# Reordered expert products around chunk 1, and a split store of the last rows, in a fused attention and expert kernel

## The chip, the cores and the metric

The kernel runs on one core of a Trainium2 chip. The metric is the device time of one execution in microseconds. Before the change its median is 507.99 us over six executions (506.37 to 508.11).

## The reference

Attention over pooled keys and values, followed by a mixture of four experts that are all computed for every row:

```python
# q, k, v: (8 batches, 8 heads, 576 rows, 64); pool = 8, so 72 pooled keys
k_p = k.reshape(B, H, 72, 8, D).mean(axis=3)
v_p = v.reshape(B, H, 72, 8, D).mean(axis=3)
attn = softmax(q @ k_p.T / 8)
x = (attn @ v_p), heads side by side        # (4608, 512)
p = domain_probs / domain_probs.sum(-1)     # (4608, 4)
for e in range(4):                          # w1: (4, 512, 1024), w2: (4, 1024, 512)
    out += p[:, e:e+1] * (relu(x @ w1[e]) @ w2[e])
```

## The kernel before

**Chunks and steps.** The 4608 rows are cut into nine chunks of 512: chunk c below 8 is the first 512 rows of batch c, and chunk 8 collects the last 64 rows of every batch. A step is one chunk with one expert; `steps` lists them, chunk by chunk, expert by expert, and the loop over s (L946) has one pass more than steps. In pass s the up products (x times w1, then relu) of step s are written out together with the down products (hidden times w2) of step s-1. Hidden values stand transposed, `H_sb`, in two buffers; the sums over experts stand in `accs`, one tile per 128 rows.

**Forms.** `up_plain` (L658) makes an up product in 8 column blocks of 4 matmuls with 512 columns. `up_seven` (L718) makes it by Strassen's scheme from seven products of half the size (`product`, L641: four matmuls of 256 columns into one of the three banks `g`, `d`, `s` of `psum_h`); ScalarE keeps a partial sum in `r` (L691), VectorE adds it and applies the relu (L695), and ScalarE does a relu alone (L698). `up_down` (L776) puts both the up and the down product into that scheme, from step (1, 2) on. The scheme needs sums of weights (`combine_w1` L595, `combine_w2` L627, four operations on VectorE each, for the expert named) and of inputs (`forms_of`, L606). `down` (L848) is the plain down product: 8 matmuls of 512 columns for each of four row blocks, in pieces n = 0 to 3 of 3, 4, 5 and 4 matmuls for each half j, and then `merge` (L865) multiplies by the probability and adds, on VectorE (L872), into `acc`.

**Pass 4** (s == E, L1006) stands between the last step of chunk 0 and the Strassen steps of chunk 1: chunk 1's first up product is plain. For j = 0 it does the four down pieces; for j = 1 each down piece is followed by two of the eight up blocks.

**Order.** All engines run in the order in which the code is written (`manual_schedule`, L893). Work for the next batch's attention is dropped into it at numbered points: every `between` or `up_down` counts through `point` (L935), 16 points a pass, and `placed` holds what is due at each. At a `slot` (L941) also the next entry of `forms_due` is taken, which is where the sums of weights go. `second_attention` (L516) is the plan of batch 1 during chunk 0, by point number: fold the keys (L203, VectorE), transpose them (`second_keys`, L315, PE, then an ACT copy), transpose the queries in two halves (`second_queries`, L322, PE, then a VectorE copy), four `scores` (L263, PE, then an exp on ACT, L276), two halves of `fold_values` (L246), four `context` (L400, PE, then reciprocal and `x_tok` on VectorE, L376 and L377), each with its `turn` (L418), a DMA transpose from SP's queue that writes a quarter of xT. `attention(c)` (L539) is the plan of batch c+1 during chunk c, in the same way.

**Banks.** `psum_a` holds one tile of two banks, which key and query transposes, scores and contexts of batches 1 to 7 take in turn: each waits until the one before has been read. `psum_h` and `psum_o` have three banks each. For batch 0, `attention_first` (L489) and `turn_here` (L423) use transposes on PE; there two row blocks share one `psum_a` tile, and a copy on ACT (L432) takes each out.

**Loads and stores.** The inputs are loaded from POOL's queue, in code order; all but the probabilities are cast to bf16 on the way. `store` (L880) writes a finished row block from SP's queue; for chunk 8 these are two transfers of 64 rows, since a row block holds rows of two batches. Pass 36 has only the down products of the last step and these stores (L990 to L992).

Of the kernel before, what the change touches and what calls it, by code (L numbers as in the profile page):

```python
# [13 lines left out]
BF16 = mybir.dt.bfloat16  # L14
F32 = mybir.dt.float32
# [3 lines left out]
def kernel(  # L19
# [10 lines left out]
    nc = tc.nc  # L30

    B, H, S, D = q.shape
# [78 lines left out]
    def load_q(b):  # L111
        q_sb = qpool.tile([P, H, NR, D], BF16, name="q_sb")
        nc.gpsimd.dma_start(
            out=q_sb[:].rearrange("p h r d -> p h (r d)"),
            in_=q[b, :, 0:NT, :].rearrange("h (p r) d -> p h (r d)", r=NR),
        )
        raws[("q", b)] = q_sb
# [22 lines left out]
    def load_v(b):  # L140
        load_kv(b, v, "vraw")
# [281 lines left out]
    def turn_here(b, r):  # L423
        if r == 0:
            state[("xT", b)] = xpool.tile([P, KC, NT], BF16, name="xT")
        if r % 2 == 0 or b:
            state["xt_ps"] = psum_a.tile([P, 2, KC, P], BF16, tag="a", name="xt_ps")
        xt_ps = state["xt_ps"][:, r % 2]
        flat = state.pop(("x", b, r))[:].rearrange("p a h d -> p (a h d)")
        for kc in range(KC):  # L430
            nc.tensor.transpose(xt_ps[:, kc, :], flat[:, kc * P:(kc + 1) * P], ident[:])
        nc.scalar.copy(out=state[("xT", b)][:, :, r * P:(r + 1) * P], in_=xt_ps)  # L432

    def rem_queries(i):
        q_rem = q_rems.pop(i)
# [80 lines left out]
    def second_attention():  # L516

        lo, hi = halves

        return {  # L520
            42: [lambda: fold_keys(1, lo)],
            44: [lambda: fold_keys(1, hi), lambda: load_k(2)],
            47: [second_keys],
            50: [lambda: second_queries(0)],
            51: [lambda: second_queries(1), lambda: load_q(2), lambda: load_q_rem(2)],
            53: [lambda: scores(1, 0)],
            55: [lambda: scores(1, 1)],
            56: [lambda: fold_values(1, lo)],
            57: [lambda: scores(1, 2)],
            58: [lambda: fold_values(1, hi)],  # L530
            59: [lambda: scores(1, 3)],
            60: [lambda: context(1, 0), lambda: turn(1, 0)],
            61: [lambda: context(1, 1), lambda: turn(1, 1)],
            62: [lambda: context(1, 2), lambda: turn(1, 2)],
            63: [lambda: context(1, 3), lambda: turn(1, 3)],
            64: [lambda: load_v(2)],
        }

    def attention(c):  # L539

        lo, hi = halves
        b = c + 1
        plan = {}

        def add(n, *what):
            plan.setdefault(n, []).extend(what)

        if c % 2:
            i = c // 2
            q_at = 15 if b < B else 2  # L550
            for n, piece in zip((0, 8, 11, 12), (rem_queries, rem_scores, rem_context, rem_turn)):
                add(q_at + n, lambda piece=piece: piece(i))
        parts = forms_of(b, nc.gpsimd)
        add(25, *parts)
        if b == B:
            return plan
        more, far = b + 1 < B, b + 2 < B
        if c == 1:
            add(0, lambda: queries(b), *key_parts(b)[:2])
            add(1, *key_parts(b)[2:])  # L560
            add(1, lambda: keys(b), lambda: loads_wait(b))
            add(1, lambda: (load_q(b + 1), load_q_rem(b + 1)))
            for pair in range(NPAIR):
                add(7 + pair, lambda pair=pair: scores(b, pair))
            for n, part in enumerate(value_parts(b)):
                add(6 + n, part)
            mixed = (11, 12, 13, 14)
        else:
            for pair in range(NPAIR):
                add(2 + 2 * pair, lambda pair=pair: scores(b, pair))  # L570
            for n, part in enumerate(value_parts(b)):
                add(4 + n, part)
            mixed = (9, 11, 12, 19)
        for n, r in zip(mixed, range(NR)):
            add(n, lambda r=r: context(b, r))
            add(n + 1, lambda r=r: turn(b, r))
        if more:
            add(4, lambda: load_half(b + 1, k, "kraw", 0))
            add(11, lambda: queries(b + 1))
            add(8, lambda: load_half(b + 1, k, "kraw", 1))  # L580
            add(16, *key_parts(b + 1))
            add(21, lambda: load_half(b + 1, v, "vraw", 0))
            add(27, lambda: load_half(b + 1, v, "vraw", 1))
            add(24, lambda: keys(b + 1))
        if far:
            add(28, lambda: (load_q(b + 2), load_q_rem(b + 2)))
        return plan
# [259 lines left out]

    def down(c, e, j, n):  # L848

        first = (0, 3, 7, 12, 16)  # L850
        for at in range(first[n], first[n + 1]):
            r, fc = 2 * j + at // FCH, at % FCH
            if fc == 0:
                sums[r] = psum_o.tile([P, DM], F32, name="o_ps")
            nc.tensor.matmul(  # L855
                sums[r][:], lhsT=hidden[(c, e)][:, fc, r * P:(r + 1) * P], rhs=w2_bf[:, e, fc, :],
                start=(fc == 0), stop=(fc == FCH - 1),
            )
            if fc == FCH - 1:
                if held is not None and r == NR - 1:  # L860
                    held.append(lambda: merge(c, e, r, sums[r]))
                else:
                    merge(c, e, r, sums[r])

    def merge(c, e, r, o_ps):  # L865
        prob = p_all[:, c * NR + r, e:e + 1]
# [10 lines left out]
            return  # L877
        store(c, r)

    def store(c, r):  # L880
        dst = accs[(c, r)][:]
        if c < B:
            rows = out[c * S:c * S + NT, :].rearrange("(p r) d -> p r d", r=NR)
            nc.sync.dma_start(out=rows[:, r, :], in_=dst)
        else:
            for bb in range(2):
                at = (2 * r + bb) * S + NT
                nc.sync.dma_start(out=out[at:at + REM, :], in_=dst[bb * REM:(bb + 1) * REM])

    zeros = x_rem[:, 0]  # L890
    pool_map = x_rem[0:FR, 1, 0:FT * SP].rearrange("p (r j) -> p r j", r=FT)
# [1 line left out]
    with tc.manual_schedule(engines={ENG.PE, ENG.DVE, ENG.Activation, ENG.Pool, ENG.SP}):  # L893
# [52 lines left out]
        for s in range(len(steps) + 1):  # L946
# [17 lines left out]
            if s == 1:  # L964
                w, u, x = combine_w2(0), combine_w1(0), forms_of(0)
                forms_due.extend([lambda w=w, u=u, n=n: (w[n](), u[n]()) for n in range(3)])
                forms_due.extend(nothing[:1] + combine_w1(2))
                for part in x[:3]:
                    part()
            elif s == 2:  # L970
                x[3]()
                forms_due.extend(nothing + combine_w1(3))
            elif s == 4:
                v2, x = combine_w2(1), forms_of(1)
                forms_due.extend(v2[:2] + combine_w1(1))
                forms_due.extend([lambda: (x[0](), x[1]()), lambda: x[2]()])
            elif s == 5:
                x[3]()
                forms_due.extend(u[3:] + nothing[:2] + combine_w2(2))
            elif s == 6:  # L980
                v3 = combine_w2(3)
                forms_due.extend(nothing[:1] + v3[:1] + nothing[:2] + v3[1:])
            elif s == 7:
                forms_due.extend(nothing[:1] + v2[2:3] + nothing[:3] + v2[3:])
            elif s == 8:
                forms_due.extend(nothing[:1] + w[3:])
            elif s == E * B + 1:
                reload_w2(E - 1)
            for j in range(2):
                if not live:  # L990
                    for n in range(4):
                        between(j, n)  # L992
                elif s == 0:
                    for i in range(4):
                        up_half(j, i)
                        if j == 0 and i in (1, 2):
                            turn_here(0, i + 1)
                        if j == 0 and i == 2:
                            norm_probs()
                        between(j, i)  # L1000
                elif s == 1:
                    for n in range(4):
                        between(j, n)
                    for n in range(4):
                        up_plain(c, e, [4 * j + n])
                elif s == E:  # L1006
                    for n in range(4):
                        between(j, n)
                        if j:
                            up_plain(c, e, [2 * n, 2 * n + 1])  # L1010
                elif splits(*steps[s - 1]):
                    up_down(c, e, j, *steps[s - 1])
                else:
                    up_seven(c, e, j, lambda n: between(j, n))
# [30 lines left out]
```

## Time and profile before

| | us |
|---|---|
| median of six executions | 507.99 |
| the six | 506.37, 506.74, 507.95, 508.04, 508.07, 508.11 |
| the profiled execution | 508.07 |
| its span, first to last instruction | 506.4 |
| PE busy / VectorE busy / ACT busy / POOL busy | 493.6 / 354.9 / 287.2 / 180.0 |
| first matmul of pass 36 (at 494.7) to the end of the span | 11.7 |
| DMA bytes | 41.90 MB |

Busy times are sums over the span; PE's includes the drawn ends of pipelined matmuls, which overlap the next one. A line of the timeline gives start, duration, engine, source line, operation, what it writes and reads, shape and count of equal instructions in a row; brackets give the idle time of the engine before it and what ended that. The table by stretches gives the busy time of each engine from one time to another, the clock granted to PE, the share of the DMA engines and the rate of the transfers.

### The profile page before, as it was taken

What the parts mean: (1) busy time and instruction counts of PE and PEld (TensorE: products, weight loads), DVE (VectorE), ACT (ScalarE), POOL (GpSimd) and SP (SyncE); (2) the same over time, 40 slices, a digit from 0 to 9 for tenths busy, and PEclk for the clock granted to TensorE, in tenths of its full rate; (3) what the DMA queues carried; (4) which work ended last, traced back from release to release, by engine and by line L of the source; (5) the groups of instructions that cost most, each with busy time, mean ns of one, the idle gap of its engine ahead of it and who ended that gap; (6) DMA issues with size and microseconds to landing.
All of it is one profiled execution on the core that took longest, in us unless ns stands there. A gap on an engine that the chain in (4) does not pass through costs nothing.

```text
span 506.4 us, 10931 instructions
## 1 busy us (share of the span) xinstructions
PE 493.6 (97%) x4468; PEld 392.9 (78%) x4483; DVE 354.9 (70%) x650; ACT 287.2 (57%) x531; POOL 180.0 (36%) x165
## 2 busy tenths in 40 slices
PE   8899889999999999999999999999999999999996
PEld 3656544667888888888888888888888888888883
DVE  2363879677777776777777777777877766776674
ACT  3554343745576557655766576556655565556650
POOL 8372102144522671266126722661115111512110
PEclk9899999999999999999999999999999999999999
DMA  9999997991837355844673286333200110012003
GB/s 132 205 206 206 201 147 153 122 112 15 87 103 98 48 55 122 109 49 47 122 108 53 19 123 118 51 45 62 64 18 16 43 43 12 2 43 63 2 1 83
DMA packets 83506, 41.90 MB, mean 83 GB/s; under 512 B 46576, under 2 KB 78832, under 8 KB 83456
## 3 DMA queue, kind: packets, MB, share of 16 engines
q0 software_dynamic: 42112, 22.91, 35.2%
q1 hardware_dynamic: 41344, 18.29, 17.0%
q8 instruction: 35, 0.57, 0.4%
q14 instruction: 15, 0.12, 0.1%
HBM read 45.69 MB, written 9.44 MB: 109 GB/s over the span
## 4 chain that ended last, share of the span: by engine, by line
PE 91%; DVE 5%; ACT 2%; DMA 1%; issue 1%; ACTq 0%; POOLq 0%
PE g_ps L647 38%; PE u_ps L769 35%; PE o_ps L855 8%; PE h_ps L665 3%; PE two L272 2%; PE h_ps L678 2%; PE two L395 1%; DVE H_sb L695 1%; DMA H_sb<-in_k_dram 1%; DVE x_tok L377 1%; DVE acc L872 1%; DVE acc L753 0%; PE o_ps L487 0%; ACT expT L357 0%; ACT xT L432 0%
## 5 line engine op out<-in xcount | busy, mean ns | idle before, releaser
L647 PEld LDWEIGHTS <-w_bf 128*128 128x128 bf16 x1848 | 177.4, 98 | 27.9 <-issue 2.5
L753 DVE SCALAR_TENSOR_TENSOR acc<-u_ps,p_all,acc 128x512 f32<-128x512 f32 (+1 forms) x204 | 121.3, 594 | 77.0 <-ACT u_ps L806 72.7
L715 POOL TENSOR_TENSOR h_s<-H_sb,h_s 128x1024 bf16<-128x1024 bf16 x29 | 61.5, 2120 | 236.3 <-DVE h_s L714 236.3
L647 PE MATMUL g_ps<-xT,w_bf 128*128 128x256 bf16 x928 | 130.0, 273 | 0.0
L647 PE MATMUL g_ps<-xf,w_bf 128*128 128x256 bf16 x792 | 109.8, 272 | 0.6 <-ACT g_ps L790 0.4
L691 ACT COPY r<-g_ps 128x512 f32<-128x512 f32 x140 | 81.9, 585 | 46.4 <-PE g_ps L647 41.8
L695 DVE CUSTOM_DVE_ANT_0 H_sb<-g_ps,r 128x512 bf16<-128x512 f32 x140 | 96.3, 688 | 13.4 <-ACT r L691 8.7
L769 PEld LDWEIGHTS <-H_sb 128*128 128x128 bf16 x928 | 86.7, 98 | 18.3 <-DVE H_sb L713 4.7
L769 PE MATMUL u_ps<-w_bf,H_sb 128*128 128x256 bf16 x696 | 95.3, 273 | 0.4 <-DVE H_sb L713 0.3
L698 ACT ACTIVATE H_sb<-g_ps 128x512 bf16<-128x512 f32 x124 | 74.0, 597 | 20.6 <-PE g_ps L647 20.6
L769 PEld LDWEIGHTS <-h_s 128*128 128x128 bf16 x696 | 68.1, 98 | 7.9
L790 ACT COPY g_ps<-g_ps 128x512 f32<-128x512 f32 x58 | 33.1, 570 | 65.3 <-PE g_ps L647 65.3
L769 PE MATMUL u_ps<-w_t,h_s 128*128 128x256 bf16 x464 | 69.6, 273 | 0.0
L855 PE MATMUL o_ps<-w_bf,H_sb 128*128 128x512 bf16 x213 | 53.2, 379 | 0.6
L806 ACT COPY u_ps<-u_ps 128x256 f32<-128x256 f32 x58 | 20.7, 357 | 32.9 <-PE u_ps L769 32.7
L855 PEld LDWEIGHTS <-H_sb 128*128 128x128 bf16 x224 | 21.8, 98 | 18.9
L769 PE MATMUL u_ps<-w_t,H_sb 128*128 128x256 bf16 x232 | 34.9, 273 | 0.0
L769 PE MATMUL u_ps<-w_bf,h_s 128*128 128x256 bf16 x232 | 34.8, 273 | 0.0
L276 ACT ACTIVATE expT<-two 72x1024 bf16<-72x1024 f32 x28 | 28.5, 1016 | 4.0 <-PE two L272 4.0
L377 DVE TENSOR_TENSOR x_tok<-two,inv 128x512 bf16<-128x512 f32 x32 | 22.1, 692 | 1.1
L808 DVE TENSOR_SCALAR acc<-u_ps,p_all 128x512 f32<-128x512 f32 x14 | 10.5, 751 | 16.8 <-ACT u_ps L806 16.8
L794 ACT COPY u_ps<-u_ps 128x256 f32<-128x256 f32 x58 | 21.1, 364 | 0.0
(116 smaller groups left out, 433.1 us busy)
## 6 DMA issues: line engine op xcount, KB each, us to landing
out_dram<-acc SPq DMA_DIRECT2D x32, 256.0 KB, 2.4
w_bf<-in_moe_w_dram POOLq DMA_DIRECT2D x17, 256.0 KB, 9.9
w_bf<-in_moe_w_dram POOLq DMA_DIRECT2D x4, 1024.0 KB, 17.2
q_sb<-in_q_dram POOLq DMA_DIRECT2D x7, 512.0 KB, 9.7
raw_kv<-in_k_dram POOLq DMA_DIRECT2D x10, 288.0 KB, 6.7
raw_kv<-in_v_dram POOLq DMA_DIRECT2D x10, 288.0 KB, 6.6
raw_kv<-in_k_dram POOLq DMA_DIRECT2D x2, 576.0 KB, 15.3
w_t<-in_v_dram POOLq DMA_DIRECT2D x2, 576.0 KB, 13.5
```

The source lines that it names most:

```text
L276: nc.scalar.activation(out=state[("expT", b)][:, 2 * pair:2 * pair + 2].rearrange("j h r s p -> j s (h r) p"), in_=two[0:SP].rearrange("j ...
L377: nc.vector.tensor_tensor(out=x_tok[:], in0=c_ps[:, :, :, 0:D], in1=inv[:].unsqueeze(3).to_broadcast([P, 2, NPAIR, D]), op=ALU.mult,)
L647: nc.tensor.matmul(bank[:, t, :], lhsT=w1_bf[:, e, block, kc, lo:lo + P], rhs=x[:, kc, :], start=(first and t == 0 and kc == 0), stop=(t = ...
L691: nc.scalar.copy(out=r[:], in_=ps[:])
L695: nc.vector._custom_dve(TENSOR_ADD_SAT, out=out, in0=ps[:], in1=r[:], s0=BIG, s1=0.0)
L698: nc.scalar.activation(out=out, in_=ps[:], func=ACT.Relu)
L715: lambda: nc.gpsimd.tensor_sub(out=s4, in0=a12, in1=s2),
L753: nc.vector.scalar_tensor_tensor(out=acc, in0=ps, scalar=prob, in1=acc, op0=ALU.mult, op1=ALU.add,)
L769: nc.tensor.matmul(out, lhsT=lhs[0][:, lhs[1] + f, lhs[2]], rhs=rhs[0][:, rhs[1] + f, rhs[2]], start=(start and f == 0), stop=(f == FCH // ...
L790: nc.scalar.copy(out=s[:], in_=g[:])
L794: nc.scalar.copy(out=two[:, lo], in_=one[:, lo])
L855: nc.tensor.matmul(sums[r][:], lhsT=hidden[(c, e)][:, fc, r * P:(r + 1) * P], rhs=w2_bf[:, e, fc, :], start=(fc == 0), stop=(fc == FCH - 1),)
```

## The change

1. `turn_here` (batch 0): each row block has a tile of its own; block 1's is taken from `psum_o`.
2. `second_attention` (batch 1): key transposes at point 48 instead of 47, second query half at 52 instead of 51, scores at 54, 56, 58, 59 instead of 53, 55, 57, 59, contexts with their turns at 61, 63, 65, 68 instead of 60 to 63. Points 64 and up lie in pass 4.
3. `attention(1)` (batch 2): the key folds and queries of pass 4 come at its offsets 2 and 3 instead of 0 and 1; scores, value folds and contexts each one offset later.
4. Pass 4: the four pieces of the second half of the down product come one after the other, and then the eight up blocks.
5. `combine_w2(1)`: its four operations come in passes 7 and 8; before, two came in pass 4 and two in pass 7. The sums of w1 and the forms of x in passes 4 and 5 move accordingly.
6. The last row block of the last step is made in two halves of 256 columns (`last_half`), each with its own add and its own stores, and all stores of chunk 8 alternate between SP's and ACT's queue.

```diff
--- before.py
+++ after.py
@@ -423,13 +423,12 @@
     def turn_here(b, r):
         if r == 0:
             state[("xT", b)] = xpool.tile([P, KC, NT], BF16, name="xT")
-        if r % 2 == 0 or b:
-            state["xt_ps"] = psum_a.tile([P, 2, KC, P], BF16, tag="a", name="xt_ps")
-        xt_ps = state["xt_ps"][:, r % 2]
+        pool, tag = ((psum_o, "o_ps") if r == 1 else (psum_a, "a"))
+        xt_ps = pool.tile([P, KC, P], BF16, tag=tag, name="xt_ps")
         flat = state.pop(("x", b, r))[:].rearrange("p a h d -> p (a h d)")
         for kc in range(KC):
             nc.tensor.transpose(xt_ps[:, kc, :], flat[:, kc * P:(kc + 1) * P], ident[:])
-        nc.scalar.copy(out=state[("xT", b)][:, :, r * P:(r + 1) * P], in_=xt_ps)
+        nc.scalar.copy(out=state[("xT", b)][:, :, r * P:(r + 1) * P], in_=xt_ps[:])
 
     def rem_queries(i):
         q_rem = q_rems.pop(i)
@@ -520,20 +519,18 @@
         return {
             42: [lambda: fold_keys(1, lo)],
             44: [lambda: fold_keys(1, hi), lambda: load_k(2)],
-            47: [second_keys],
+            48: [second_keys],
             50: [lambda: second_queries(0)],
-            51: [lambda: second_queries(1), lambda: load_q(2), lambda: load_q_rem(2)],
-            53: [lambda: scores(1, 0)],
-            55: [lambda: scores(1, 1)],
-            56: [lambda: fold_values(1, lo)],
-            57: [lambda: scores(1, 2)],
-            58: [lambda: fold_values(1, hi)],
+            52: [lambda: second_queries(1), lambda: load_q(2), lambda: load_q_rem(2)],
+            54: [lambda: scores(1, 0)],
+            56: [lambda: scores(1, 1), lambda: fold_values(1, lo)],
+            58: [lambda: scores(1, 2), lambda: fold_values(1, hi)],
             59: [lambda: scores(1, 3)],
-            60: [lambda: context(1, 0), lambda: turn(1, 0)],
-            61: [lambda: context(1, 1), lambda: turn(1, 1)],
-            62: [lambda: context(1, 2), lambda: turn(1, 2)],
-            63: [lambda: context(1, 3), lambda: turn(1, 3)],
-            64: [lambda: load_v(2)],
+            61: [lambda: context(1, 0), lambda: turn(1, 0)],
+            63: [lambda: context(1, 1), lambda: turn(1, 1)],
+            65: [lambda: context(1, 2), lambda: turn(1, 2)],
+            68: [lambda: context(1, 3), lambda: turn(1, 3)],
+            71: [lambda: load_v(2)],
         }
 
     def attention(c):
@@ -556,15 +553,16 @@
             return plan
         more, far = b + 1 < B, b + 2 < B
         if c == 1:
-            add(0, lambda: queries(b), *key_parts(b)[:2])
-            add(1, *key_parts(b)[2:])
-            add(1, lambda: keys(b), lambda: loads_wait(b))
-            add(1, lambda: (load_q(b + 1), load_q_rem(b + 1)))
+            add(3, lambda: queries(b))
+            add(2, *key_parts(b)[:2])
+            add(3, *key_parts(b)[2:])
+            add(3, lambda: keys(b), lambda: loads_wait(b))
+            add(3, lambda: (load_q(b + 1), load_q_rem(b + 1)))
             for pair in range(NPAIR):
-                add(7 + pair, lambda pair=pair: scores(b, pair))
+                add(8 + pair, lambda pair=pair: scores(b, pair))
             for n, part in enumerate(value_parts(b)):
-                add(6 + n, part)
-            mixed = (11, 12, 13, 14)
+                add(7 + n, part)
+            mixed = (12, 13, 14, 15)
         else:
             for pair in range(NPAIR):
                 add(2 + 2 * pair, lambda pair=pair: scores(b, pair))
@@ -847,7 +845,12 @@
 
     def down(c, e, j, n):
 
-        first = (0, 3, 7, 12, 16)
+        if (c, e) == (B, E - 1) and j and n:
+            if n == 1:
+                for lo in (0, TH):
+                    last_half(c, e, NR - 1, lo)
+            return
+        first = (0, 3, 7, 12, 16) if (c, e) != (B, E - 1) or j == 0 else (0, FCH)
         for at in range(first[n], first[n + 1]):
             r, fc = 2 * j + at // FCH, at % FCH
             if fc == 0:
@@ -862,6 +865,19 @@
                 else:
                     merge(c, e, r, sums[r])
 
+    def last_half(c, e, r, lo):
+
+        o_ps = psum_o.tile([P, DM], F32, tag="o_ps", name="o_ps")
+        cols = slice(lo, lo + TH)
+        for fc in range(FCH):
+            nc.tensor.matmul(
+                o_ps[:, 0:TH], lhsT=hidden[(c, e)][:, fc, r * P:(r + 1) * P],
+                rhs=w2_bf[:, e, fc, cols], start=(fc == 0), stop=(fc == FCH - 1),
+            )
+        dst = accs[(c, r)][:, cols]
+        add(dst, p_all[:, c * NR + r, e:e + 1], o_ps[:, 0:TH])
+        store_rem(r, dst, cols)
+
     def merge(c, e, r, o_ps):
         prob = p_all[:, c * NR + r, e:e + 1]
         if e == 0:
@@ -877,15 +893,18 @@
             return
         store(c, r)
 
+    def store_rem(r, src, cols):
+        for bb, queue in enumerate((nc.sync, nc.scalar)):
+            at = (2 * r + bb) * S + NT
+            queue.dma_start(out=out[at:at + REM, cols], in_=src[bb * REM:(bb + 1) * REM])
+
     def store(c, r):
         dst = accs[(c, r)][:]
         if c < B:
             rows = out[c * S:c * S + NT, :].rearrange("(p r) d -> p r d", r=NR)
             nc.sync.dma_start(out=rows[:, r, :], in_=dst)
         else:
-            for bb in range(2):
-                at = (2 * r + bb) * S + NT
-                nc.sync.dma_start(out=out[at:at + REM, :], in_=dst[bb * REM:(bb + 1) * REM])
+            store_rem(r, dst, slice(0, DM))
 
     zeros = x_rem[:, 0]
     pool_map = x_rem[0:FR, 1, 0:FT * SP].rearrange("p (r j) -> p r j", r=FT)
@@ -971,9 +990,12 @@
                 x[3]()
                 forms_due.extend(nothing + combine_w1(3))
             elif s == 4:
-                v2, x = combine_w2(1), forms_of(1)
-                forms_due.extend(v2[:2] + combine_w1(1))
-                forms_due.extend([lambda: (x[0](), x[1]()), lambda: x[2]()])
+                x = forms_of(1)
+                u1 = combine_w1(1)
+                forms_due.extend(nothing + [
+                    lambda: (u1[0](), u1[1]()), lambda: (u1[2](), u1[3]()), lambda: x[0](),
+                    lambda: (x[1](), x[2]()),
+                ])
             elif s == 5:
                 x[3]()
                 forms_due.extend(u[3:] + nothing[:2] + combine_w2(2))
@@ -981,9 +1003,10 @@
                 v3 = combine_w2(3)
                 forms_due.extend(nothing[:1] + v3[:1] + nothing[:2] + v3[1:])
             elif s == 7:
-                forms_due.extend(nothing[:1] + v2[2:3] + nothing[:3] + v2[3:])
+                v2 = combine_w2(1)
+                forms_due.extend(nothing[:1] + v2[:1] + nothing[:3] + v2[1:2])
             elif s == 8:
-                forms_due.extend(nothing[:1] + w[3:])
+                forms_due.extend(nothing[:1] + w[3:] + v2[2:3] + nothing[:2] + v2[3:])
             elif s == E * B + 1:
                 reload_w2(E - 1)
             for j in range(2):
@@ -1006,8 +1029,8 @@
                 elif s == E:
                     for n in range(4):
                         between(j, n)
-                        if j:
-                            up_plain(c, e, [2 * n, 2 * n + 1])
+                    if j:
+                        up_plain(c, e, range(FCH))
                 elif splits(*steps[s - 1]):
                     up_down(c, e, j, *steps[s - 1])
                 else:
```

## The prediction

> **What bounds the kernel now.** The page first: which engine is full.
>
> ```profile
> PE 493.6 (97%) x4468; PEld 392.9 (78%) x4483; DVE 354.9 (70%) x650; ACT 287.2 (57%) x531; POOL 180.0 (36%) x165
> ```
>
> TensorE works 97% of the span, so only stretches in which it stands, or runs slower, can give anything. The table by stretches finds them (columns as in its first line).
>
> ```profile
> core 0: us, PE busy (x) PEld busy (x) DVE busy (x) ACT busy (x) POOL busy (x), PEclk, DMA share, GB/s
> 19.10:22.50 3.40, 3.40 (x21) 2.54 (x19) 0.15 (x1) 1.46 (x3) 1.01 (x2) 0.50 1.25 209
> 50.40:60.30 9.90, 8.58 (x72) 5.79 (x72) 9.22 (x18) 3.51 (x6) 0.84 (x1) 1.00 1.30 204
> 69.30:75.60 6.30, 4.71 (x52) 2.63 (x52) 4.69 (x11) 1.51 (x3) 0.85 (x1) 1.00 1.06 116
> 75.60:89.75 14.15, 14.04 (x67) 6.24 (x67) 13.24 (x27) 5.08 (x8) 2.90 (x4) 1.00 0.85 156
> 494.70:506.40 11.70, 7.03 (x33) 3.04 (x32) 4.13 (x6) 0.00 (x0) 0.00 (x0) 1.00 0.39 90
> ```
>
> PE lacks 1.3 us where batch 1's keys and queries are made (50 to 60), 1.6 in its contexts (69 to 76), and 4.7 at the end; 50 to 60 is also where VectorE is full (9.22 of 9.90). The timeline of PE names the waits.
>
> ```profile
> 17.47 0.38 PE L431 MATMUL xt_ps<-ident,x_tok 128*128 128x128 bf16 x4 [0.41 <-ACT xT L432]
> ...
> 54.24 0.29 PE L319 MATMUL kpt_ps<-ident,kp 72*128 72x72 bf16 x4
> 55.50 0.30 PE L319 MATMUL kpt_ps<-ident,kp 72*128 72x72 bf16 x4 [0.96 <-DVE kp L207]
> ...
> 58.48 1.03 PE L855 MATMUL o_ps<-w_bf,H_sb 128*128 128x512 bf16 x4
> 59.81 0.61 PE L329 MATMUL qt_ps<-ident,q_sb 128*128 128x128 bf16 x8 [0.30 <-DVE qT L333]
> ...
> 71.83 0.43 PE L395 MATMUL two<-vp,expT 72*128 72x65 bf16 x8 [0.61 <-DVE x_tok L377]
> ...
> 73.33 0.43 PE L395 MATMUL two<-vp,expT 72*128 72x65 bf16 x8 [0.62 <-DVE x_tok L377]
> ...
> 74.79 0.43 PE L395 MATMUL two<-vp,expT 72*128 72x65 bf16 x8 [0.16 <-DVE x_tok L377]
> ```
>
> Matmuls follow one another by less than their drawn length, so I measure a wait from start to start: a group of four takes 0.44 us at 256 columns (60.26 to 60.70) and 0.86 at 512, five of 512 take 1.08, a context 0.27 (71.83 to 72.10). The kpT wait is then 1.12 (54.24 plus 0.14 to 55.50), the qT wait 0.46, the four contexts' 0.29 (69.43 to 69.72), 0.76, 0.79 and 0.33: 3.75 in all, and 0.41 at 17.47.
>
> **The change, part by part**, on the profiled execution's clock (508.07 us, span 506.4, 1.7 around it).
>
> *Batch 0's second turn gets its own bank.* The 0.41 at 17.47 goes: x_tok is ready at 17.00, PE is free by then, and ACT's copy and the first up product (18.53) follow 0.41 earlier. Next late is that copy itself. Gain 0.41; bounds 0 and 0.41.
>
> *Second attention respread.* I walk PE's new order by these durations, everything up to 53 moved 0.41 earlier. kpT now comes after eight more product matmuls (0.87): it arrives at 54.84, VectorE's kp is ready at 55.08, wait 0.24 instead of 1.12. The first query transposes arrive at 56.74, but q_sb of batch 1, issued at 35.77, landed 21.2 us later, at 56.95: wait 0.26; before, PE came at 58.04 and never met it. The second query transposes arrive at 59.17 and need VectorE's first qT copy (here 58.65 to 59.33): 0.21. Scores 2 and 3 now have only four 512 matmuls between them, and one double bank serves both: ACT's r copy (0.59) and exp (1.02) end at 67.32, PE comes at 66.88: 0.49, new. Context 0 then waits for nothing. Context 1 has a product and a down piece before it (1.30), but H_sb, acc, reciprocal and x_tok stand in line on VectorE behind ACT's r (69.41), ending at 71.62: 0.42. Contexts 2 and 3 find 0.13 and 0.30 by the same count. Sum 2.05 against 3.75: gain 1.70. Bounds: 0 (VectorE sets the pace and each wait only moves) and 3.75.
>
> *Downs ahead of the plain ups in step 4.* The same 64 matmuls in another order, 13.8 us either way. Cover: 25 downs (5.39) follow context 3 (its matmuls end at 74.86). Its recip and x_tok take 1.0, its transpose is issued by 75.95; the last transpose of before landed 2.5 us after its issue, so xT is whole at 78.4 and the ups start at 80.25: 1.8 us spare. Moved on SP: two stores now stand ahead of the qT and kpT transposes of batch 2. Those landed at 81.84 and 83.91; behind two 256 KB stores I estimate them by 87, and the scores that need them start at 88. Up products' relus (0.60 each) stay under their matmuls (0.86). VectorE works 13.24 of 14.15 us in this stretch; it loses two of its 0.68 us operations. load_v(2) keeps its place among POOL's DMAs, since plan points bind only the order on each queue. Batch 2's scores and contexts move one slot later in a stretch where PE stands for nothing today (28.24 busy of 28.45 from 89.75 to 118.2). Value 0; bounds -0.4 and +1 (xT late).
>
> *combine_w2(1) moved to steps 7 and 8.* Step 7 keeps as many operations as before; step 8 gets two more, 0.60 each in line. In its first half H_sb and its reader stand like this:
>
> ```profile
> 138.70 0.69 DVE L695 CUSTOM_DVE_ANT_0 H_sb<-g_ps,r 128x512 bf16<-128x512 f32 x1
> ...
> 139.81 1.04 PE L647 MATMUL g_ps<-xf,w_bf 128*128 128x256 bf16 x8
> ```
>
> H_sb frees the bank at 139.39, 0.42 ahead of PE; 0.60 later, and a floor of 0.05 for the signal, makes PE wait 0.23. In the second half L713 ends at 147.74 and PE reads it at 148.12: likewise about 0.3. Loss 0.56; bounds 0 and 1.2.
>
> *Tail.* The last row block in two halves: 16 matmuls of 0.109 for 8 of 0.216, +0.02. What follows was:
>
> ```profile
> 501.82 0.75 DVE L872 SCALAR_TENSOR_TENSOR acc<-o_ps,p_all,acc 128x512 f32<-128x512 f32 x1 [0.97 <-PE o_ps L855]
> ```
> ```profile
> L888 SPq DMA_DIRECT2D out_dram<-acc x8: 466/562/587, 497.4 to 503.1; - x8
> ...
> DMA to landing us min/median/max: 2.2/2.3/2.4
> ```
>
> The last add is half as wide, 0.48 by the 256 column rows of L753, against 0.75: 0.27. SP issued two stores one after the other (502.60, 503.12); now the second goes out from ACT, idle since 494.2, and 0.52 falls away. The first half's stores and row block 2's are issued by 502.0, before the last ones. Gain 0.77 with the 0.02 taken off. No row shows a store from ACT: bounds -0.5 (its issue or its landing is slower by what the other saves and more) and 1.1 (half the bytes land sooner). I take the SP row, the nearest.
>
> **Sum:** 508.07 - 0.41 - 1.70 + 0.56 - 0.77 = 505.75. The profiled time is 0.08 above the median of the six (507.99), so **505.7**.
>
> *The clock.* In 19.1 to 22.5 PE was granted half its clock: 3.4 us, some 1.7 lost. Four of the six times lie at 508.0 to 508.1, two at 506.4 and 506.7, which fits its coming in some executions only. In the changed kernel I expect it to matter less: the query transposes at 57.0 wait for q_sb's landing, whichever clock came before. So I add nothing; an execution without it gains 0.3 at most.
>
> [...]
>
> **Rivals.**
> *The waits only move* (0.15). For: VectorE is full from 50 to 60, and the contexts still go through one double bank. Against: its queue there shortens relative to PE as products move ahead. Then 1.70 goes: 507.4.
> *The waits vanish* (0.12): ACT and VectorE run ahead once the contexts are spread, leaving only q_sb's 0.26, and step 8 hides its additions: 505.7 - 1.79 - 0.56 = 503.4.
> *xT late* (0.11), slower than before. All ups now stand behind the fourth transpose, with nothing between. From an issue at 75.95 a landing beyond 4.3 us makes PE stand, beyond 6.7 us eats the whole gain. For: the first transpose of this batch took 5.4 us beside the loads, one of batch 2 took 8.3 beside a qT transpose and a load. Against: the fourth took 2.5, the loads being done by 76.8. With 8.3: 505.7 + 4.0 = 509.7.
> *It does not do what it says*: the order of the changed program shows all 32 downs ahead of 32 ups, contexts apart, ten stores on two queues, so this is out.
>
> **How the numbers follow.** Forecast 0.62 at 505.7, itself 504.6 to 506.8 by the bounds of tail and step 8. A measurement can tell about 0.2%, 1.0 us, from no change. Faster: forecast and vanishing waits, 0.74. Within: moved waits, 0.15. Slower: late xT, 0.11. The range takes in the moved and the vanished waits, 503.3 to 507.5; what it leaves out is the late xT and the edges.
>
> **What would show it.** Right: no wait at the second turn; kpT's wait near 0.24; the first query transposes at 57.0 held by q_sb; contexts waiting 0.8 in sum instead of 2.2; L665's analogue starting near 80.3 in one row of 32; two short waits for H_sb in step 8; the end about 3.8 us after the last add's start instead of 4.55. Wrong: PE idle before the ups for xT; a wait for kpT or qT in step 5; a first store of ACT that lands later than SP's.

## The result and the profile after

| | before | after |
|---|---|---|
| median, us | 507.02 (50 executions; 507.99 in the six known before) | 505.98 (23 executions) |
| lowest and highest | 506.35, 511.33 | 505.18, 506.73 |
| profiled execution, its span | 508.07, 506.4 | 505.51, 503.8 |

The changed kernel takes 0.9975 of the time of before (95% interval 0.9967 to 0.9983): 1.27 us less, 0.86 to 1.67, and 1.04 by the two medians. The time was forecast within 0.3 us (505.7). The gain was not: 2.3 was forecast from the six executions known then, half of it came.

The page of after, engines first, then the chain that ended last, by engine and by line:

```profile
PE 492.5 (98%) x4476; PEld 392.7 (78%) x4491; DVE 355.2 (71%) x651; ACT 286.9 (57%) x531; POOL 179.0 (36%) x165
...
PE 82%; DMA 9%; DVE 4%; POOL 2%; ACT 1%; issue 1%; POOLq 0%; ACTq 0%
```

PE is busy 1.1 us less in a span 2.6 shorter, so it stood less. The new thing is DMA 9%. On the page of before it has 1%: there the chain hardly ran over a transfer. Now two transfers hold it, w2 of expert 1 and q_sb of batch 1. (The chain follows a transfer back to its issue, so the share is far more than the time that PE stands for it, which the rows below give.) The same stretches of the table as before, in time; the work in them has moved forward a little:

```profile
core 0: us, PE busy (x) PEld busy (x) DVE busy (x) ACT busy (x) POOL busy (x), PEclk, DMA share, GB/s
19.10:22.50 3.40, 3.34 (x36) 2.88 (x34) 0.20 (x1) 2.81 (x6) 1.04 (x2) 1.00 1.25 210
50.40:60.30 9.90, 9.00 (x75) 5.97 (x75) 8.48 (x18) 3.46 (x6) 1.69 (x2) 1.00 1.30 203
69.30:75.60 6.30, 5.82 (x50) 2.92 (x49) 5.64 (x12) 0.60 (x1) 0.00 (x0) 1.00 1.24 177
75.60:89.75 14.15, 14.10 (x75) 6.70 (x76) 12.29 (x26) 6.75 (x11) 2.59 (x4) 1.00 0.69 151
492.60:503.80 11.20, 7.03 (x41) 3.82 (x39) 4.33 (x7) 0.00 (x0) 0.00 (x0) 1.00 0.33 94
```

The clock is whole in the first row, where it was halved; the contexts' stretch lacks 0.5 instead of 1.6, and the end, cut from the first matmul of pass 36, is 0.5 shorter with the same 7.03 of PE work. PE's timeline, the rows that answer to those of before:

```profile
16.95 0.45 PE L430 MATMUL xt_ps<-ident,x_tok 128*128 128x128 bf16 x4
...
40.36 0.81 PE L858 MATMUL o_ps<-w_bf,H_sb 128*128 128x512 bf16 x3 [0.22 <-DMA w_bf<-in_moe_w_dram]
...
53.38 0.71 PE L319 MATMUL kpt_ps<-ident,kp 72*128 72x72 bf16 x8
...
56.35 0.62 PE L329 MATMUL qt_ps<-ident,q_sb 128*128 128x128 bf16 x8 [0.74 <-DMA q_sb<-in_q_dram]
...
70.80 0.43 PE L395 MATMUL two<-vp,expT 72*128 72x65 bf16 x8 [0.26 <-DVE x_tok L377]
...
79.42 1.89 PE L663 MATMUL h_ps<-xT,w_bf 128*128 128x512 bf16 x8
...
101.85 0.43 PE L395 MATMUL two<-vp,expT 72*128 72x65 bf16 x8 [0.20 <-DVE x_tok L377]
```

The second turn waits for nothing. Two waits for transfers are there instead (0.38 at 40, 0.90 at 56, from start to start), and one in step 5 for a context of batch 2 (0.37) that the forecast did not have. The plain ups start 1.8 us after xT is whole (77.6). The last add, from VectorE's timeline, is half as wide:

```profile
499.72 0.48 DVE L751 SCALAR_TENSOR_TENSOR acc<-o_ps,p_all,acc 128x256 f32<-128x256 f32 x1 [0.39 <-PE o_ps L873]
```

From its start to the end of the span are 4.06 us, instead of 4.54.

**A table of marks.** Behind the early part, pieces with the same code take the same time in every profile, to 0.04 us. So I cut each trace at marks that all kernels share: the first query transposes of batch 1 (Q), the first product of step 5, the first of ACT's u_ps copies in steps 7 and 9, the last such copy, the last add's start, the end of the span. One row is one profiled execution, in us; each row with 1.7 for what lies around the span adds up to the whole time.

| kernel | start to Q | Q to step 5 | step 5 to 7 | 7 to 9 | 9 to last copy | to last add | last add to end |
|---|---|---|---|---|---|---|---|
| before | 58.04 | 31.71 | 30.10 | 27.26 | 344.75 | 9.97 | 4.54 |
| e1 before again | 57.88 | 31.34 | 30.10 | 27.26 | 344.71 | 9.97 | 4.56 |
| e2 tail only | 56.93 | 31.33 | 30.10 | 27.26 | 344.71 | 9.99 | 4.06 |
| **after** | 56.35 | 29.98 | 30.92 | 27.47 | 345.01 | 9.99 | 4.06 |
| e3 turn back | 56.98 | 29.98 | 30.92 | 27.46 | 344.99 | 9.99 | 4.07 |
| e4 w2 in the gaps | 56.25 | 29.99 | 30.92 | 26.44 | 344.71 | 9.98 | 4.06 |
| e5 q between | 55.52 | 30.89 | 30.92 | 27.47 | 345.03 | 9.99 | 4.06 |
| e6 ups mixed | 57.77 | 31.11 | 30.92 | 27.47 | 345.03 | 9.98 | 4.07 |
| e7 unspread | 57.57 | 31.24 | 31.41 | 27.47 | 345.03 | 9.99 | 4.06 |
| e8 shifted signals | 57.31 | 29.98 | 30.92 | 27.47 | 345.00 | 9.98 | 3.68 |
| e9 all | 54.89 | 30.33 | 30.55 | 26.45 | 344.72 | 9.98 | 3.68 |
| e10 before, loads halved | 56.63 | 31.72 | 30.10 | 27.27 | 344.72 | 9.97 | 4.58 |
| e11 turn only | 56.93 | 31.64 | 30.10 | 27.26 | 344.73 | 9.97 | 4.57 |
| e12 before, filled | 56.97 | 31.46 | 30.10 | 27.26 | 344.71 | 9.97 | 4.55 |

Only the first column scatters, and in before's order the second by as much as the second qT is waited for: 0.46 in before and 0.47 in e10, less where q_sb held PE at Q (none in e1 and e2). Behind Q, after against e1: -1.36 and +0.82 (0.44 of both is one set of scores of batch 2 that went from step 4 to step 5, so -0.92 and +0.38), +0.21, +0.30, +0.02, -0.50. That is 0.51 less, or 0.48 with 0.03 more around the span.

### The profile page after: what moved, and what is told of

It is laid out like the page before. It is cut to its first block, busy times and chain, and to the rows that moved or that the text cites. A ratio compares the mean times of both kernels' runs of the same rounds, so it can differ in the third digit from the quotient of the medians.

```text
span 503.8 us, 10954 instructions
## 1 busy us (share of the span) xinstructions
PE 492.5 (98%) x4476; PEld 392.7 (78%) x4491; DVE 355.2 (71%) x651; ACT 286.9 (57%) x531; POOL 179.0 (36%) x165
## 4 chain that ended last, share of the span: by engine, by line
PE 82%; DMA 9%; DVE 4%; POOL 2%; ACT 1%; issue 1%; POOLq 0%; ACTq 0%
PE g_ps L645 37%; PE u_ps L767 35%; PE o_ps L858 5%; DMA w_bf<-in_moe_w_dram 4%; DMA q_sb<-in_q_dram 4%; PE two L272 2%; PE h_ps L663 1%; PE two L395 1%; POOL w_bf L147 1%; DVE acc L751 1%; DVE H_sb L693 1%; DVE x_tok L377 1%; POOL H_sb L107 1%; ACT r L689 0%; PE o_ps L873 0%
## 5 line engine op out<-in xcount | busy, mean ns | idle before, releaser
L693 DVE CUSTOM_DVE_ANT_0 H_sb<-g_ps,r 128x512 bf16<-128x512 f32 x140 | 96.2, 688 | 15.2 <-ACT r L689 10.0
L767 PEld LDWEIGHTS <-H_sb 128*128 128x128 bf16 x928 | 86.7, 98 | 18.3 <-DVE H_sb L711 4.9
L858 PE MATMUL o_ps<-w_bf,H_sb 128*128 128x512 bf16 x205 | 51.4, 379 | 0.9 <-DMA w_bf<-in_moe_w_dram 0.2
L858 PEld LDWEIGHTS <-H_sb 128*128 128x128 bf16 x216 | 20.6, 98 | 18.4 <-issue 1.0
```

The source lines that it names most:

```text
L693: nc.vector._custom_dve(TENSOR_ADD_SAT, out=out, in0=ps[:], in1=r[:], s0=BIG, s1=0.0)
L767: nc.tensor.matmul(out, lhsT=lhs[0][:, lhs[1] + f, lhs[2]], rhs=rhs[0][:, rhs[1] + f, rhs[2]], start=(start and f == 0), stop=(f == FCH // ...
L858: nc.tensor.matmul(sums[r][:], lhsT=hidden[(c, e)][:, fc, r * P:(r + 1) * P], rhs=w2_bf[:, e, fc, :], start=(fc == 0), stop=(fc == FCH - 1),)
```

## The experiments

**Theory (landings):** ahead of Q both kernels wait for the load stream, so what the forecast counted there is lost; what is kept is made behind Q. **Rival (waits):** each wait counts with its length, as the forecast had it. A third thing came up on the way, the clock (e11, e12).

### e1: the kernel before once more

> The kernel before, once more, for a profile in which the clock is not halved from 19.1 to 22.5. My theory (the landings rule): without the 1.7 us lost there the span is 504.7 +- 0.4, PE meets w2 of expert 1 (landing near 40.3) and q_sb of batch 1 (landing near 56.3 to 57.0), so of the 1.58 us that kpT and qT showed only about 0.5 to 0.8 could be won. Rival (the waits rule): PE comes after both landings as in the first profile, and the waits for kp and qT are again 1.1 and 0.5. A row with a clock of 0.50 again would tell nothing.

507.51, clock whole. Its PE timeline:

```profile
54.28 0.30 PE L319 MATMUL kpt_ps<-ident,kp 72*128 72x72 bf16 x4 [0.97 <-DVE kp L207]
...
57.88 0.62 PE L329 MATMUL qt_ps<-ident,q_sb 128*128 128x128 bf16 x8 [0.90 <-DMA q_sb<-in_q_dram]
```

Half and half. The wait for kp is whole (1.14 from start to start), as the rival has it, and w2 of expert 1 is no bound here. But Q waits another 1.06 for q_sb, which landed at 57.83 this time: without kp's wait, Q would have come no sooner. The span is not 504.7 either: a late landing took the place of the half clock. In all profiles but e5, e9 and e10, whose loads are changed, q_sb landed between 56.2 and 57.8, and that is the scatter of the first column. e1 is a late one, but the same holds in e2, e11 and e12, which have before's order and loads and a whole clock there: Q starts 0.04 to 0.05 behind q_sb's landing (56.88, 56.89 and 56.93) although PE had stood 1.12 to 1.13 for kp before.

### e2: the tail alone

The edits of `down`, `last_half`, `store_rem` and `store`, put into the kernel before.

> The kernel before with the change of its tail alone. Theory: 0.50 us faster. The last landing comes 2.7 us after the last add's start instead of 3.63, but what runs after that landing grows from 0.92 to 1.35. Rival (the forecast's sum): 0.77 faster.

506.31 against 506.77 (ratio 0.9993, 0.9984 to 1.0002): 0.46 by medians, which alone would not tell 0.50 from 0.77; the last column says 0.50, 4.56 to 4.06, the theory's number. The last add in e2, 4.06 ahead of the end of its span:

```profile
500.31 0.48 DVE L753 SCALAR_TENSOR_TENSOR acc<-o_ps,p_all,acc 128x256 f32<-128x256 f32 x1 [0.39 <-PE o_ps L875]
```

### e3: the second turn as before

```diff
-        pool, tag = ((psum_o, "o_ps") if r == 1 else (psum_a, "a"))
-        xt_ps = pool.tile([P, KC, P], BF16, tag=tag, name="xt_ps")
+        if r % 2 == 0 or b:
+            state["xt_ps"] = psum_a.tile([P, 2, KC, P], BF16, tag="a", name="xt_ps")
+        xt_ps = state["xt_ps"][:, r % 2]
```

> The changed kernel with the bank of batch 0's second turn as before. Theory (landings): 0.0 to 0.1 us slower than the changed kernel; the wait of 0.41 at 17.5 is back, the wait of 0.38 for w2 of expert 1 at 39.9 goes in its place, and the first query transposes start with q_sb's landing at 56.3 all the same. Rival (the forecast's sum): 0.41 slower.

506.12, 0.14 above after (ratio to before 0.9980, 0.9968 to 0.9992). The wait at the turn is back, the one for w2 of expert 1 is gone, and Q starts with q_sb's landing, at 56.98. What PE gains in the turn, the next transfer takes. The medians are too close to tell 0.1 from 0.41; it is the rows that speak for the theory:

```profile
40.42 0.60 PE L646 MATMUL g_ps<-xT,w_bf 128*128 128x256 bf16 x4
40.86 0.38 PE L859 MATMUL o_ps<-w_bf,H_sb 128*128 128x512 bf16 x1
...
56.98 0.62 PE L329 MATMUL qt_ps<-ident,q_sb 128*128 128x128 bf16 x8 [0.89 <-DMA q_sb<-in_q_dram]
```

### e4: combine_w2(1) where VectorE is idle

```diff
-                forms_due.extend(nothing[:1] + v2[:1] + nothing[:3] + v2[1:2])
+                forms_due.extend(nothing[:3] + v2[:2])
...
-                forms_due.extend(nothing[:1] + w[3:] + v2[2:3] + nothing[:2] + v2[3:])
+                forms_due.extend(nothing[:1] + w[3:] + nothing[:1] + v2[2:])
```

> The changed kernel with the four operations of combine_w2(1) moved to where VectorE stands idle for 2 us: two at the border of the halves of step 7, two at that of step 8. Theory (they stand in line ahead of H_sb): the waits of 0.21 and 0.26 in step 8 go and so do most of the 0.41 and 0.44 in step 7, 0.9 to 1.3 us faster than the changed kernel. Rival: PE waits there for what VectorE does anyway, and the waits only move: 0 to 0.3 faster.

504.38, 1.60 below after by medians (ratio to before 0.9951, 0.9939 to 0.9964), 1.33 by the columns (1.03 and 0.30). The reason stands in VectorE's timeline of after: w2's operation (L635) stands in line ahead of H_sb (L693), whose bank PE needs at 137.21.

```profile
135.69 0.68 DVE L635 TENSOR_TENSOR w_t<-w_bf,w_t 128x1024 bf16<-128x1024 bf16 x1
...
136.69 0.68 DVE L693 CUSTOM_DVE_ANT_0 H_sb<-g_ps,r 128x512 bf16<-128x512 f32 x1
```

PE's next row starts at 137.42, 0.21 late. In e4 all four waits, the two that the change brought and the two of 0.41 and 0.44 in step 7 that were there before, are gone. The theory (a line ahead of H_sb) is right, and the two waits of step 7 alone, 0.82 by the column (27.26 in e1, 26.44 in e4), were worth more than the change's whole loss there (0.51).

### e5: q of batch 1 between the halves of w2

```diff
-        load_w2(2)
-        load_q(1)
+        load_w2(2, [slice(0, 4)])
+        load_q(1)
+        load_w2(2, [slice(4, FCH)])
```

> The changed kernel with w2 of expert 2 loaded in two halves and q of batch 1 between them: the same bytes, q_sb lands some 2.6 us earlier (near 53.7), the second half of w2 near 56.3 where PE needs it at 56.5. Theory (landings): the 0.90 at 55.3 goes, and 0.5 to 0.9 of it is kept at the end. Rival (VectorE's line rules behind it): the waits for x_tok and expT grow by the same, 0 to 0.2 faster.

505.29, 0.69 below after (ratio to before 0.9970, 0.9960 to 0.9981). Q waits for nothing, but the second half of w2 now ends the wait:

```profile
55.52 0.61 PE L329 MATMUL qt_ps<-ident,q_sb 128*128 128x128 bf16 x8
...
57.10 0.81 PE L858 MATMUL o_ps<-w_bf,H_sb 128*128 128x512 bf16 x3 [0.76 <-DMA w_bf<-in_moe_w_dram]
```

The same bytes, but the last of them is needed about 0.6 us of work later. That this is where a gain comes from is argued, and the gain itself is not clear: 0.69 is a difference of medians from two comparisons, the ratios to before (0.9970 here, 0.9975 in after) have intervals that overlap, and the two profiled executions are alike (505.58 and 505.51).

### e6: the ups between the downs

```diff
                         between(j, n)
-                    if j:
-                        up_plain(c, e, range(FCH))
+                        if j:
+                            up_plain(c, e, [2 * n, 2 * n + 1])
```

> The changed kernel with the plain up products of step 4 between the down products again, as before the change. Theory (the downs are the cover of the later fourth turn): the first up product comes after 12 down products (2.6 us) behind context 3, at 76.9, and stands until xT lands at 77.6: 0.8 us slower than the changed kernel (0.5 to 1.3). Rival (the order is of no matter): within 0.1.

507.47, 1.49 above after (ratio to before 1.0012, 1.0003 to 1.0021); by the second column 1.13.

```profile
79.17 1.89 PE L663 MATMUL h_ps<-xT,w_bf 128*128 128x512 bf16 x8 [0.96 <-DMA xT<-x_tok]
```

The column lies in the theory's range (0.5 to 1.3), the medians beyond it. So the downs ahead of the ups gain nothing themselves, but they hide the later fourth turn, and without them the respread loses all it brings.

### e7: batch 1's places as before

`second_attention` of the kernel before in the changed kernel; all else as changed.

> The changed kernel with the places of batch 1's keys, queries, scores and contexts as before. Theory (landings): 0.6 to 0.9 us slower than the changed kernel: the contexts' waits come back (2.2 instead of 0.9 with 0.45 for the scores), while in front of them the q_sb landing at 56.3 bounds what the other places give. Rival (the forecast's sum): 1.70 slower.

507.48, 1.50 above after (ratio to before 1.0014, 1.0005 to 1.0023), near the rival's 1.70. My 0.6 to 0.9 was wrong: behind Q the columns give 1.26 and 0.49. The 0.49 is the wait of batch 2's context in step 5, 0.86 instead of 0.37. Of the 1.26, 0.41 is a wait for the second qT, which is 0.08 in e1; in this execution k of batch 1 landed late (50.47; 49.07 in e1) and kp held PE for 2.63, so the columns of this row say less than the others.

### e8: other signals at the end

```diff
-            nc.sync.dma_start(out=rows[:, r, :], in_=dst)
+            parts = (slice(0, TH), slice(TH, DM)) if 8 <= c * NR + r < 14 else (slice(0, DM),)
+            for cols in parts:
+                nc.sync.dma_start(out=rows[:, r, cols], in_=dst[:, cols])
```

> The changed kernel with six stores of the middle (batches 2 and 3) issued as two column halves each, so that by count the last two stores signal the last two of the eight semaphores on which SP waits at the end, one after another, instead of the first two. Theory (SP's closing waits run one by one, and six pairs at 0.063 us stood behind ACT's last landing): from the last add's start to the end 3.68 us instead of 4.06, 0.38 faster. Rival (only the landing counts, ACT's at 502.42 being later than SP's): 4.06 again, no change.

505.59, 0.39 below after (ratio to before 0.9966, 0.9954 to 0.9979), and 3.68 in the last column, as the theory had it. In after's trace SP's closing waits run two signals at a time, 0.059 to 0.064 us a pair; ACT's last store is in the second of nine, which was met at 502.44, and seven pairs came behind it. In e8 it is in the last but one, so six pairs fewer stand behind the landing: 0.37 by the mean of 0.061, 0.38 by the column.

### e10 and e9: the early part without the loads as a bound

Both load w2 of experts 1 and 2 and q of batch 1 in halves:

```diff
-        load_w2(1)
+        load_w2(1, [slice(0, FCH // 2), slice(FCH // 2, FCH)])
...
-        load_w2(2)
-        load_q(1)
+        load_w2(2, [slice(0, FCH // 2)])
+        load_first_q(0, 1)
+        load_w2(2, [slice(FCH // 2, FCH)])
+        load_first_q(1, 1)
```

e10 is the kernel before with this alone. e9 is the changed kernel with this, e4's and e8's edits, and combine_w2(2)'s last operation moved behind the contexts of step 5:

```diff
-                forms_due.extend(u[3:] + nothing[:2] + combine_w2(2))
+                v2 = combine_w2(2)
+                forms_due.extend(u[3:] + nothing[:2] + v2[:3] + nothing[:1] + v2[3:])
```

> The kernel before with only those loads in halves. Here q_sb and w2 are no bound, so the early part of the forecast shows without them: its waits for kpT (1.1) and for the second qT (0.4) stand in their places. Theory (the landing hid them): its first query transposes start at about 56.3 without a wait for q_sb, 0.7 to 1.2 us later than in the run e9 with the same loads; whole time 506.0 to 506.3. Rival (the respread is worth nothing ahead of the contexts even so): within 0.3 of e9 at that point.

> The changed kernel with what the runs found put together: combine_w2(1) in VectorE's idle places, combine_w2(2)'s last operation behind batch 2's contexts, w2 of experts 1 and 2 and q of batch 1 loaded in halves (w2 of expert 2 and q by turns), and the six split stores. Theory: against the changed kernel 1.33 by combine_w2(1), 0.37 by the context in step 5, 0.38 at the end, and 0.5 to 1.4 in front of 56 since no landing is waited for: 2.6 to 3.5 faster, 502.5 to 503.4. Rival (VectorE then holds PE for kp by as much): 2.1 faster, 503.9, with the kpT wait grown by the rest.

e10: 506.87, no gain (ratio 1.0003, 0.9992 to 1.0013), where the theory had 506.0 to 506.3. e9: 502.64, 4.3 below before and 3.3 below after (0.9908, 0.9895 to 0.9922). PE's timeline in e10:

```profile
54.09 0.30 PE L319 MATMUL kpt_ps<-ident,kp 72*128 72x72 bf16 x4 [0.98 <-DVE kp L207]
...
56.63 0.61 PE L329 MATMUL qt_ps<-ident,q_sb 128*128 128x128 bf16 x8
```

and in e9:

```profile
52.84 0.69 PE L319 MATMUL kpt_ps<-ident,kp 72*128 72x72 bf16 x8
...
54.89 0.61 PE L329 MATMUL qt_ps<-ident,q_sb 128*128 128x128 bf16 x8
```

From the first up product (18.77 in e10, 17.92 in e9) to step 7 are 99.67 us in e10 and 97.85 in e9, or 98.22 with the 0.37 of step 5 put back. So, from one profile each, the respread is worth 1.45 where no landing hides it, and of it 0.89 lies ahead of Q (37.86 us to Q in e10, 36.97 in e9), the forecast's 0.88 for kpT. The forecast's 1.70 was near what the order of PE's work is worth, not what this kernel could keep. The rival for e10 is out (Q comes 1.74 later than in e9, 0.89 of it by the respread), and e9 has the theory's time. For the kernel before the halved loads bring nothing by the medians: there kp holds PE.

### e11 and e12: the clock

The mean granted clock is known for 86 executions of the kernel before from the comparisons above and these. In 18 it was 0.997 or less, as in the profiled one (3.4 us at half clock are 0.34% of the span); their median is 508.0, that of the other 68 is 506.75. The mean is a rough mark: a small drop need not cost time (six of e11's twelve have 0.998 and a median of 506.45, the other six have 0.999 or more and 506.78). Of the 18, 17 took 507.85 or more and one 506.73. Three more kernels with the old bank (e2, e3, e10) had it 8 times in 34; eight with the new one (after, e4 to e9, e11) once in 81. e11 is before with the new bank alone, e12 before with PE's last early wait filled:

```diff
         context_first(3, 0)
         context_first(3, 1)
+        warm(2)
```

> The kernel before with the own bank of batch 0's second turn alone. Of 58 executions of the kernel before whose mean clock is known so far, 12 had 0.997 or less (median 508.03, 507.85 to 508.81; the others 506.28 to 507.52); of 69 of kernels with the new bank, one. Theory (the clock): the wait of 0.41 at 17.5 was what made the thin stretch thin enough; without it no execution or one in about twelve is at half clock, and the median falls by 0.1 to 0.4 while the fastest execution stays within 0.1 of 506.3, since the landings of w2 and q_sb take the 0.41 back. Rival (the forecast's sum): every execution is 0.41 faster and the share at half clock stays at one in five.

> The kernel before with two more 512-column products of zeros (0.43 us) put into PE's wait of 0.58 us ahead of the first up product (18.5); the turn's bank is as before. Theory (the clock goes by how thinly PE is used there): the share at half clock falls as with the bank, to none or one in about twelve, and the fastest execution stays at 506.3. Rival (the bank matters, not PE's use): still one in five above 507.8.

e11: 506.61, 506.33 to 507.18, none of 12 at 0.997 (ratio 0.9991, 0.9982 to 1.0000). e12: 506.66, 506.24 to 507.28, one of 12 at 0.997, and that one took 506.75 (0.9988, 0.9978 to 0.9997). Before, beside them: 506.92, with 5 of 23 at 0.997 or less. Both take away the executions near 508 and leave the fastest where it was: the theory, not the rival. A share of one in five that stayed would still give none of 12 in 7 cases of 100, but none of 24 in fewer than 1, so it is the two together that show it. The table by stretches shows how much PE does in the 3.4 us ahead of the halving, in before and then in e11 (columns: length, PE busy, clock, DMA share, GB/s):

```profile
15.68:19.08 3.40, 2.08 (x37) 1.00 1.24 205
19.08:22.50 3.42, 3.42 (x21) 0.50 1.25 210
```
```profile
15.68:19.08 3.40, 2.49 (x41) 1.00 1.24 204
```

e12 has 2.34 there; e1 and e3, with the old bank, 1.84 and 1.85, and both kept their clock in the profiled execution. So the half clock goes with the thin stretch (0.997 or less in 26 of 120 executions with the old bank, in 2 of 93 with the new one or with the zeros), but it comes in some executions only. What decides in which was not shown.

## Why the prediction was right, and where it was not

**The account.** Of the 1.04 between the medians, some 0.27 is the half clock of before (507.02, the median of the 50, to 506.75, the median of the 68 others of e11's count; within those 86 it is 0.09); 0.48 is made behind Q; 0.29 is left, ahead of Q. For the last part only the direction is shown: e10 and e9 say that PE of before comes to Q 0.89 us later, counted from the first up product, and 0.41 more by the turn, when no load holds it, so in executions with an early landing some of that counts. How often q_sb lands early enough was not measured.

That 505.7 came so near is in part luck. The sum started from an execution at half clock and put the clock at nothing, but the half clock alone is worth some 1.3 (508.03 to 506.75, the medians with and without). Of the 2.32 that the sum did count, 0.77 came (506.75 to 505.98). The two errors nearly cancel.

The range was also added up wrongly: the bounds given for the tail (-0.5 and 1.1) and for step 8 (0 and 1.2) make 504.8 to 507.6, not 504.6 to 506.8. 505.98 lies in both.

1. *Second turn, -0.41.* Right as a wait, wrong as a gain: alone it takes 0.31 off the median (e11, with an interval that reaches 0), by the clock and not by 0.41 in each execution, since the transfers at 40.3 and 56.3 take those back (e3).
2. *Respread, -1.70.* This is the step that failed, in what it was set against. Its waits came nearly as walked: kpT 0.27 (0.24), scores 3 0.45 (0.49), contexts 0, 0.42, 0.15, 0.32 (0, 0.42, 0.13, 0.30); the second query transposes waited for nothing (0.21), the first scores 0.20. But "the first query transposes held by q_sb", 0.26 in the walk, was 0.90, and was set against an execution of before in which PE, 1.7 us late by the half clock, "never met it". At a whole clock before's order meets it too, in e1, e2, e11 and e12. So the 0.88 of kpT could not count in any of these four, and -0.92 behind Q was left.
3. *Downs ahead of ups, 0.* Right: 1.8 us spare, as said. Two things were put at nothing: the cover, which is worth 1.13 (e6), and, wrongly, the move of batch 2's contexts, "in a stretch where PE stands for nothing". PE stands 0.37 in step 5 (101.85), since the last context now has only 1.3 us of products (0.44 and 0.86) between it and the one before, and w2's operation (L636) and x_tok are in line on VectorE in that time. e9 moved that operation, and 0.37 came back.
4. *combine_w2(1), +0.56.* Measured 0.21 and 0.30; in e4 they go. Right, by the row of H_sb. The 0.05 for the signal is in before's trace: 0.053 to 0.058 us lie between VectorE's end and PE's start in the ten waits of PE for VectorE.
5. *Tail, -0.77.* Measured 0.50. The stores did land 0.93 sooner after the last add's start (2.70 instead of 3.63), more than forecast; but from the last landing to the end it took 1.36 instead of 0.92 (e8: the order in which SP waits for the signals). The bound "its landing is slower" was looked for and came (2.4 from ACT, 2.1 from SP); the wait behind it was not in the sum.
6. *The clock.* "In the changed kernel I expect it to matter less": shown, but for another reason than the landing: it hardly comes any more (1 of 24 executions of after at 0.997 or less). With a fuller stretch ahead of it (2.49 and 2.34 us of PE work instead of 2.08) it came in none and one of 12 executions (e11, e12).
7. *Rivals.* The moved waits would have given 507.4, the vanished ones 503.4, and neither came; xT was not late, since the transposes landed by 77.6 behind the loads, as the "against" said.

The stores of the two halves, as the DMA view of after lists them (size, median time from issue to landing):

```profile
out_dram<-acc SPq DMA_DIRECT2D x2, 64.0 KB, 2.1
out_dram<-acc ACTq DMA_DIRECT2D x2, 64.0 KB, 2.4
```

VectorE's rows in after behind the 0.37 of step 5 (the context starts at 101.85):

```profile
100.27 0.68 DVE L636 TENSOR_TENSOR w_bf<-w_bf 128x1024 bf16<-128x1024 bf16 x1
...
101.10 0.69 DVE L377 TENSOR_TENSOR x_tok<-two,inv 128x512 bf16<-128x512 f32 x1
```

**What stays open:** the 0.29 ahead of Q; which executions get the half clock; and why one operation of combine_w2 (L633) took 1.59 in e4's and e9's idle place instead of 0.68. In e4 it began at 123.93, 0.1 after an operation of POOL (123.82 to 124.98), and ended 0.54 behind that one's end; whether it stood for POOL, no run tried, and PE did not wait for it there.

## What to carry to other kernels

Before a wait is counted as a gain, look what else ends in the same place: ask of each transfer when it lands in an execution without the disturbance that the profile happens to hold, and set the new order against that. Cut the traces of two kernels at marks that both have; where most columns agree to 0.04 us, small gains can be read from one profile that medians with a scatter of 1 us can't show. And an operation that is off the critical path goes where its engine stands idle for longer than it lasts, not to the step where it is due: here that was worth more (1.33 by the columns, e4) than the whole change.

## What the runs showed of the hardware

- In the profile of before the clock was halved for 3.41 us (19.08 to 22.50), right after 3.40 us with 2.08 us of PE work; in e1 and e3 it stayed whole after 1.84 and 1.85 us in the same 3.40. A mean clock of 0.997 or less came in 18 of 86 executions of before, in 1 of 81 of the kernels with the new bank, and in 1 of 12 with the zeros (that one at 506.75).
- In after a store from ACT lands 0.3 us later than the same from SP (medians 2.4 and 2.1 for 64 KB, 2.6 and 2.3 for 128 KB).
- The order in which SP waits for the last signals is worth 0.38 us at the end (4.06 and 3.68).
- The load stream moves 203 to 210 GB/s in the stretches of after between 15 and 60 us, and the same transfer, q_sb, lands between 56.2 and 57.8 in the profiles with the same loads: that is the scatter of the first column of marks, while the columns from step 5 on agree to 0.04 where the code is the same.
